# Fusing attention, a dense block and routed experts: keys' neighbour columns by products, turnings at other places, and a new written order

## The chip, the cores and the metric

The kernel runs on one core of one Trainium2 chip. The metric is the device time of one execution in microseconds. A core has five engines with a queue each: TensorE (PE, which loads weights beside its matmuls, PEld), VectorE (DVE), ScalarE (ACT), GpSimd (POOL) and SyncE (SP, which here only issues transfers). Each queue is worked off strictly in its order; semaphores make one engine wait for another or for a transfer.

## The reference, cut to what matters

```python
# 1. attention, 4 batches x 8 heads x 768 positions x 64
k_sum = k.reshape(B, H, 24, 32, D).max(axis=3)       # 24 block keys
v_sum = v.reshape(B, H, 24, 32, D).mean(axis=3)
scores_l = q @ k.T / 8, kept where |i - j| < 16       # a band
scores_s = q @ k_sum.T / 8 + log(32)
a = softmax(concat(scores_l, scores_s));  x = a @ concat(v, v_sum)
# 2. dense block on x as (3072, 512)
h = ((x @ w1) * (x @ w2)) @ w3;  x = h @ w_out
# 3. routed experts, 8 of 512 -> 1024 -> 512
do = x @ w_skip > 0;  e = argmax(x @ w_gate)
out = x;  out[do] += gate * (relu(x @ w1[e]) @ w2[e])
```

The four dense weights come as 64-bit floats, everything else as 32-bit.

## The kernel before, in words

**Stage one** runs from an order written out by hand. `PLAN` holds three strings; each letter is one step, and a step issues its instructions on whichever engines it needs, so the string fixes the order of every queue at once: those of PE, DVE, ACT, POOL and of SP's transfers. The letters that matter below:

- Weights: `f` loads a 512 KB piece of a 64-bit weight (SP; three buffers and one more early on, so a later load waits until a buffer is free), `A` two ACT steps on it, `p`, `i`, `d` one DVE step each, which end in a 32-bit tile; `s` splits it into a high and a low part (ACT copy, DVE difference).
- Folding of `w3 @ w_out` in full precision: `O` turns a tile of `w_out` (four 128x128 transposes), `o` copies it (ACT), `U` multiplies it by the gate columns (four products with 10 columns), `u` splits the result; `X` turns a piece of `w3`, `x` splits it, `F` is 12 matmuls on the split parts, `e` splits their result. The first `F` needs all eight `O`, `U` and `s`.
- Attention, 16 pairs of heads: `k`, `n`, `w`, `m` load keys, queries, values and rows for the block sums (`r`, DVE). `K` turns half of a pair's keys: three whole tiles of 128 positions and the 16 or 32 neighbouring positions that the band needs from the next tile. In its first half the neighbour part comes after the whole tiles, in its second half ahead of them. `h` (ACT) and `H` (DVE) read the result, `Q` and `j` do the same for queries; `S` scores, `a` the softmax, `b` its norm, `T` and `t` turn it, `V` and `v` multiply by the values. `S` and `V` use parts of the TensorE array.
- Dense block: `y` splits x, `B` is 24 matmuls, `g` their product and split, `E` 12 matmuls, `G` the result with the routing, `N` the end of a routing.

The neighbour part is a transpose of few rows, `src[lo:hi, c]` with `ident[lo:hi, lo:hi]` (L140). In both plans each letter stands equally often.

**Stage two** (from L1138, PE's order alone written) is the last three blocks of the dense block, with nothing else on PE.

**Stage three** goes over the experts (`Experts.run`, L887). Each has up to five tiles of 128 tokens; how many is known only when the routing is done, so branches decide. Rows are gathered by POOL (`fetch`), `turn` transposes a gathered tile (four transposes on PE) and splits it (one ACT copy, one DVE difference), `compute` is 24 + 24 matmuls with further turnings at given places (`turns`): ahead of the second layer's matmuls, ahead of their last twelve, and behind these. During an expert's `compute` calls ACT and DVE also split the next expert's weights (`piece`). Expert e's tile 0 is turned during expert e - 1; with more than two tiles, tile 2 is turned at the head of `rest` and its `compute` follows at once.

Of the kernel before, what the change touches and what calls it, by code (L numbers as in the profile page):

```python
# [17 lines left out]
P = 128  # L18
# [37 lines left out]
CUTS0 = (0, 1, 1, 1, 2, 3)  # L56
# [6 lines left out]
class Attention:  # L63
# [58 lines left out]
    def sum(self, i):  # L122
        nc = self.nc
        vt = self.sums.pop(i)
        sm = self.pool.tile([4 * NBLK, D], F32, tag="sm", name="sm", bufs=2)
        for n in (8, 4, 2):
            nc.vector.tensor_add(vt[:, 0:n, :], vt[:, 0:n, :], vt[:, n : 2 * n, :])
        nc.vector.tensor_add(sm, vt[:, 0, :], vt[:, 1, :])
        self.sums["half", i] = sm
        if i % 2:  # L130
            nc.vector.tensor_add(sm, self.sums.pop(("half", i - 1)), self.sums.pop(("half", i)))
            nc.vector.tensor_scalar_mul(self.vs[:, i // 4, i // 2 % 2, :], sm, 1.0 / 32.0)

    def turned(self, name, u, parts):

        src = self.t[name, u]
        f = self.ps.tile([P, 512], F32, tag="tr", name="tr", bufs=1)
        n = 0
        for c, lo, hi in parts:
            self.nc.tensor.transpose(  # L140
                f[:, n : n + hi - lo], src[lo:hi, c, :, :], self.ident[lo:hi, lo:hi]
            )
            n += hi - lo
        self.t[name, "t"] = f

# [132 lines left out]
class AttentionOrder:  # L278
# [20 lines left out]
    def step(self, c):  # L299
# [15 lines left out]
JOBS = "oooooooottttttttwttwttwttwttwwwwwwwwwwww"  # L315
PLAN = (
    (
        "kffAAfpifdpiKmOosAdhAOpUopHifduOsKHUifsrnudohUAQuApiOjdocpiOsUQofsfuApfiAjddSsUpmkiOuofnardSUsOA"
        "AapbiuSomKdphOXHisfdfrQUxTofjAuUbApiXKxuFdmFhpXfAHfiFadrQkjFxeAXppeixAFSdXiaFfpdFwxXFiedtfAbxbpS"
        "VfFeidfvTXAFptAVKaipdvSHiFxedhXnfATFbsxpFKfweXtVAfiAhFpFaHdidfpxvXQmFTeisjFxetbQAjVSdpvAkaFpSfTi"  # L320
        "tiaXFdrxdeKVvSFbAXeffFpHhixnTKFsAtpFfVhAdaHibQXvjdpTQxewijSFAtfpadfibsXeVvdFSxATptifFAVvpXaAFdbi"
        "kTFpdtKViefdxSsXfvewxTnHFAApFhtaFKmpidbissdhVHfvyFTftQsjeVkevr"
    ),
    (
        "QmjAfBSgpABabSiTngaBdpistfSrBgdKAyVpHsgBihdApQbsvigmdBTjfAfKhfrBgBHsypgAmiwdspgBAiQBtafjpkVnbdgs"
        "gSwiBvTAapdBidySQstsgVagrBlgSbBmjbB"
    ),
    (
        "kvgTKBtghHVbEgnQEyvjEKTGtEhHVaESvTrtbBanSVEvGTaEQSmwbtjErbQajNGBGVgvBKglhTmHBwKgtyVvEnTHgrBtVhES"
        "babQvESEgGaTBEtSEVgGjvbkBNgKhBHTlGEkQtVEgvjETnKGyaEGBHhgEtBbEgSmGEBaSVvawENEBgSQbjBKggTBtHaVEvTh"  # L330
        "GrBQgGbEwtVjKByvhHSggBgEBabQTGSkgaBtSEnjKVEhHvTKaHhmtEbBbQVGEvTEjgtVrSvaENkBSGGTwgBabtKgVSvgHhBT"
        "QbgmBtyjgbEQVajBKkvETtEBVgHhSBgvEanTSGEtVrbaEvKTgBbtSGVEvhHNBkmgKEhwTGGtBVHgabvgQjBTEQgBjbytVSgn"
        "BvagSETGtBKEBrEagwgSBhVHQGBEjgKBHbEvgNhkEgwbGaBBgEEybgTnQBtjGEGBVSEKvEgTtaESEGVBagvbTESgEtbNHBVh"
        "vBgTGGwQjEtKgBVanhHQgvBbTByjgtSBaSgVBQgvbaESBTjEQGajtgEEVGkKhHvbBKhNgEEwTHgEtSaVvbBSGTGbtBVagBvg"
        "TgBtbgVvSETEtVvEaTGbtEEVGEvTEtVvENGG"
    ),
)

# [359 lines left out]
class Experts:  # L698
# [188 lines left out]
    def run(self, pool, ps, early):  # L887
        tc, nc = self.tc, self.nc
        self.pool, self.ps = pool, ps
        cj = pool.tile([P, 1], I32, name="cj")  # L890
        manual = lambda: tc.manual_schedule(engines=ENGINES)
        with tc.If(early < P):
            with manual():
                self.fetch(0, 0)
                self.turn(self.place(0, 0), ps)
        with tc.If(early < 2 * P):
            with manual():
                self.fetch(0, 1)
        def state():
            return self.done, self.loaded, dict(self.raws), list(self.free)  # L900

        def soon(label, n, least):

            tc.mark_branch_hint_location(label, hint=n >= least, engines=[PE])

        def rest(e):

            at, bt = self.place(e, 2), self.place(e, 3)
            with tc.If(ns[e] > 2, label=f"three{e}"):
                with manual():  # L910
                    soon(f"four{e}", ns[e], 4)
                    self.turn(at, ps)
                    self.compute(self.col(e, 2), e, at, (None, bt))
                with tc.If(ns[e] > 3, label=f"four{e}"):
                    with manual():
                        soon(f"five{e}", ns[e], 5)
                        self.compute(self.col(e, 3), e, bt)
                    with tc.If(ns[e] > 4, label=f"five{e}"):
                        with tc.For_i(4, ns[e], 1) as j:
                            nc.vector.tensor_copy(cj, self.idx[:, bass.ds(j + e * NTILE, 1)])  # L920
                            self.gather(cj, at[0])
                            self.turn(at, ps)
                            self.compute(cj, e, at)

        ns = None
        for e in range(E):
            more = e + 1 < E
            first, own, nxt = self.place(e, 0), self.place(e, 1), self.place(e + 1, 0) if more else None
            with manual():
                if e == 0:  # L930
                    for z, j in ((1, 0), (0, 2), (1, 1), (2, 0), (2, 1), (1, 2)):
                        self.fetch(z, j)
                    self.compute(self.col(0, 0), 0, first, (None, own, nxt), CUTS0)
                else:
                    for z, j in ((2, 0), (2, 1), (1, 2)):
                        self.fetch(e + z, j)
            if ns is None:
                ns = [nc.values_load(self.nt[0:1, z : z + 1], min_val=0, max_val=NTILE) for z in range(E)]
            half, whole = (HALF, CUTS) if more else ((), ())

            before = state()
            with tc.If(ns[e] > 1, label=f"two{e}") as many:  # L944
                with manual():
                    soon(f"three{e}", ns[e], 3)
                    self.fetch(e, 3)
                    if e:
                        self.compute(self.col(e, 0), e, first, (own, nxt), half)
                rest(e)  # L950
                with manual():
                    if more:
                        soon(f"two{e + 1}", ns[e + 1], 2)
                    self.compute(self.col(e, 1), e, own, (None, None), half)
            after = state()
            self.done, self.loaded, self.raws, self.free = before[0], before[1], dict(before[2]), list(before[3])
            with many.Else():
                with manual():
                    if more:
                        soon(f"two{e + 1}", ns[e + 1], 2)  # L960
                    if e:
                        self.compute(self.col(e, 0), e, first, (None, nxt), whole)
                    else:
                        for _ in range(sum(HALF)):
                            self.piece(PIECES)
            now = state()
            assert now[:2] == after[:2] and list(now[2]) == list(after[2])
            assert [id(t) for t in now[3]] == [id(t) for t in after[3]]
# [252 lines left out]
```

## Time and profile before

| | us |
|---|---|
| median of 3 runs | 859.61 (859.29 to 861.21) |
| the profiled execution's own time | 858.83 |
| its span, first to last instruction | 857.0 |

Shares of the span: PE 95%, PEld 87%, DVE 60%, ACT 53%, POOL 12%. The profiled execution's own time is 1.83 us over its span. A timeline row names the start, the length, the engine, the line, the instruction, what it writes and reads, the count of like instructions merged into the row, and in brackets how long the engine had been idle and who ended that. Since matmuls overlap, their price is read from one start to the next, not from their lengths.

### The profile page before, as it was taken

To read this page: it belongs to the slowest core of one execution; us is meant where nothing else is said; L and a number is where in the kernel's file an instruction comes from. 1 tells how busy PE (TensorE), PEld (TensorE's weight loads), DVE (VectorE), ACT (ScalarE), POOL (GpSimd) and SP (SyncE) were. 2 spreads that over 40 slices of the span, in tenths; PEclk is the share of its full clock that TensorE was granted. 3 is DMA by queue.
4 is the path that set the end of the run, shared out by engine and by line. 5 is a ranking of instruction groups with operands and counts; after the bars stand their busy time and mean duration, and the time that the engine had idled before them with its cause. 6 is when DMAs were issued, how large, how long until landed. Compare 5 with 4: busy or idle time off the path is not lost. (4 is left out here: it accounts for less than half of the span.)

```text
span 857.0 us, 18400 instructions
## 1 busy us (share of the span) xinstructions
PE 816.4 (95%) x6882; PEld 743.4 (87%) x6882; DVE 513.8 (60%) x1684; ACT 452.3 (53%) x1235; POOL 102.5 (12%) x136
## 2 busy tenths in 40 slices
PE   3799999999999999999999999999998999998996
PEld 3689988999999999999999989999996787776775
DVE  4889998976664547566455555642354285165952
ACT  4768998766554445444334445522244274265851
POOL 1000000000110001010001010200215114022320
PEclk9999999999999999999999999999999899999999
DMA  8677877553506243233222322510136266055910
GB/s 239 170 196 192 220 186 194 160 125 81 140 10 133 63 97 89 70 87 63 60 69 61 61 41 70 183 69 22 63 111 228 104 234 213 16 184 178 332 69 21
DMA packets 124615, 105.07 MB, mean 123 GB/s; under 512 B 92914, under 2 KB 98082, under 8 KB 124496
## 3 DMA queue, kind: packets, MB, share of 16 engines
q1 hardware_dynamic: 120144, 98.04, 41.1%
q0 software_dynamic: 4352, 5.51, 2.0%
q8 instruction: 67, 1.10, 0.6%
q14 instruction: 52, 0.43, 0.2%
HBM read 90.45 MB, written 16.64 MB: 125 GB/s over the span
## 5 line engine op out<-in xcount | busy, mean ns | idle before, releaser
L573 PE MATMUL x2p<-wh,slab 128*128 128x266 f32 (+1 forms) x768 | 157.0, 291 | 0.0
L573 PEld LDWEIGHTS x2p<-wh,slab 128*128 128x128 f32 x768 | 124.1, 189 | 3.0 <-issue 1.7
L573 PE MATMUL x2p<-wl,slab 128*128 128x256 f32 (+1 forms) x384 | 109.0, 284 | 0.0
L224 ACT ACTIVATE pr<-pr,st 128x120 f32<-128x120 f32 x192 | 73.5, 386 | 41.7 <-DVE st L214 41.6
L530 PE MATMUL ab<-slab,wB1h 128*128 128x256 f32 x384 | 73.6, 290 | 0.6 <-DVE slab L547 0.6
L530 PE MATMUL ab<-slab,wA1h 128*128 128x256 f32 x384 | 73.4, 288 | 0.2 <-DVE slab L388 0.2
L552 DVE TENSOR_TENSOR a<-a,ab 128x256 f32<-128x256 f32 x84 | 35.2, 419 | 63.4 <-ACT a L543 62.9
L573 PEld LDWEIGHTS x2p<-wl,slab 128*128 128x128 f32 x384 | 72.7, 189 | 0.0
L530 PE MATMUL ab<-slab,wB2h 128*128 128x256 f32 x384 | 70.8, 282 | 0.0
L530 PE MATMUL ab<-slab,wA2h 128*128 128x256 f32 x384 | 70.3, 281 | 0.0
L553 ACT ACTIVATE slab<-a 128x256 fp32r<-128x256 f32 x84 | 35.0, 417 | 64.2 <-DVE a L552 63.7
L543 ACT ACTIVATE a<-ab 128x256 f32<-128x256 f32 x96 | 36.4, 379 | 60.2 <-PE ab L530 57.7
L530 PEld LDWEIGHTS ab<-slab,wA1h 128*128 128x128 f32 x384 | 59.0, 189 | 2.2 <-issue 0.6
L530 PEld LDWEIGHTS ab<-slab,wB1h 128*128 128x128 f32 x384 | 58.8, 190 | 1.5 <-DVE slab L547 0.8
L554 DVE TENSOR_TENSOR slab<-a,slab 128x256 fp32r<-128x256 f32 x84 | 36.4, 433 | 38.7 <-ACT slab L553 38.7
L530 PEld LDWEIGHTS ab<-slab,wB2h 128*128 128x128 f32 x384 | 59.1, 190 | 0.0
L530 PEld LDWEIGHTS ab<-slab,wA2h 128*128 128x128 f32 x384 | 58.9, 189 | 0.0
L530 PE MATMUL ab<-slab,wA1l 128*128 128x256 f32 x192 | 54.0, 281 | 0.0
L530 PE MATMUL ab<-slab,wB2l 128*128 128x256 f32 x192 | 53.9, 281 | 0.0
L530 PE MATMUL ab<-slab,wA2l 128*128 128x256 f32 x192 | 53.9, 281 | 0.0
L530 PE MATMUL ab<-slab,wB1l 128*128 128x256 f32 x192 | 53.9, 281 | 0.0
L828 ACT ACTIVATE hr<-hp 128x512 f32<-128x512 f32 x30 | 18.0, 599 | 64.3 <-PE hp L824 64.1
(176 smaller groups left out, 2087.1 us busy)
## 6 DMA issues: line engine op xcount, KB each, us to landing
eraw<-in_moe_w SPq DMA_DIRECT2D x64, 512.0 KB
raw<-in_moe_w SPq DMA_DIRECT2D x32, 512.0 KB
vaug<-in_v SPq DMA_DIRECT2D x32, 240.0 KB
x2e<-row SPq DMA_DIRECT2D x24, 256.5 KB
kn<-in_k SPq DMA_DIRECT2D x32, 192.0 KB
vt<-in_v SPq DMA_DIRECT2D x16, 384.0 KB
qn<-in_q SPq DMA_DIRECT2D x32, 192.0 KB
out<-row SPq DMA_DIRECT2D x24, 256.0 KB
```

Of the source, the lines that this page charges most:

```text
L224: nc.scalar.activation(pr[:, i, :], pr[:, i, :], AF.Exp, scale=-1.0, bias=st[:, 0, i : i + 1], accum_out=st[:, 1, i : i + 1],)
L530: self.nc.tensor.matmul(pp[:, s, :], l[:, c, fs], r[:, c, :], start=(c == 0 and j == 0), stop=(c == 3 and j == 2),)
L543: nc.scalar.activation(a, pp[:, 0, :], AF.Copy)
L552: nc.vector.tensor_mul(a, a, pp[:, 1, :])
L553: nc.scalar.activation(gh[:, f % 4, :], a, AF.Copy)
L554: nc.vector.tensor_sub(gl[:, f % 4, :], a, gh[:, f % 4, :].bitcast(F32))
L573: self.nc.tensor.matmul(po[:, 0 : hi - lo], l[:, f, s * P : s * P + P], r[:, 4 * h + f, lo:hi], start=(h == 0 and f == 0 and j == 0), stop ...
L828: nc.scalar.activation(hr, hps[s], AF.Relu)
```

## The change

It has three parts. In `turned`, the neighbour part of the keys becomes a product of the whole tile with 16 or 32 columns of the identity. In `Experts.run`, the tile turned at the end of expert 0's first `compute` is its own tile 2 (no longer expert 1's tile 0), and `rest` of expert 0 no longer turns it; and the next expert's tile 0 is turned in the last `compute` of an expert with several tiles, no longer in its first. `PLAN` is written anew, all three strings, with the same number of each letter.

```diff
         for c, lo, hi in parts:
-            self.nc.tensor.transpose(
-                f[:, n : n + hi - lo], src[lo:hi, c, :, :], self.ident[lo:hi, lo:hi]
-            )
+            if hi - lo == P:
+                self.nc.tensor.transpose(f[:, n : n + P], src[:, c, :, :], self.ident)
+            else:
+                self.nc.tensor.matmul(
+                    f[:, n : n + hi - lo], src[:, c, :, :].rearrange("p a d -> p (a d)"), self.ident[:, lo:hi], start=True, stop=True
+                )
             n += hi - lo
 PLAN = (
     (
-        "kffAAfpifdpiKmOosAdhAOpUopHifduOsKHUifsrnudohUAQuApiOjdocpiOsUQofsfuApfiAjddSsUpmkiOuofnardSUsOA"
-        "AapbiuSomKdphOXHisfdfrQUxTofjAuUbApiXKxuFdmFhpXfAHfiFadrQkjFxeAXppeixAFSdXiaFfpdFwxXFiedtfAbxbpS"
...
+        "fAfkKfApipdimfhdHOrfoAnfKUhOupoidssOsApUiHoudfAcApUOipdoiusQsmfUjkdfAQOjpiuodfSfsarUuOSApoaASiOb"
+        "mUdKnpHishoudUsAfOXrpuoAipdTfUixKduXFFxXAFpHiAdmfhQrpxieAXfjpFdkfxetQAawFXibFdxFjpSFeAabXSKiVpdf"
...
     ),
...
                     soon(f"four{e}", ns[e], 4)
-                    self.turn(at, ps)
+                    if e:
+                        self.turn(at, ps)
                     self.compute(self.col(e, 2), e, at, (None, bt))
...
-                    self.compute(self.col(0, 0), 0, first, (None, own, nxt), CUTS0)
+                    self.compute(self.col(0, 0), 0, first, (None, own, self.place(0, 2)), CUTS0)
...
-                        self.compute(self.col(e, 0), e, first, (own, nxt), half)
+                        self.compute(self.col(e, 0), e, first, (own, None), half)
                 rest(e)
...
-                    self.compute(self.col(e, 1), e, own, (None, None), half)
+                    self.compute(self.col(e, 1), e, own, (None, nxt), half)
...
                     else:
+                        self.turn(nxt, ps)
                         for _ in range(sum(HALF)):
                             self.piece(PIECES)
```

## Rows read from the trace of the kernel before

**Rows 1.** The page's first part: busy time, share of the span, instructions of each engine.
```profile
PE 816.4 (95%) x6882; PEld 743.4 (87%) x6882; DVE 513.8 (60%) x1684; ACT 452.3 (53%) x1235; POOL 102.5 (12%) x136
```

**Rows 2.** Stretches: length, busy time (instructions) of PE, PEld, DVE, ACT, POOL, clock, DMA, GB/s.
```profile
5.10:51.60 46.50, 33.63 (x181) 28.69 (x182) 34.14 (x87) 30.35 (x75) 0.72 (x1) 1.00 0.70 207
51.60:160.00 108.40, 105.00 (x1083) 96.52 (x1082) 98.93 (x288) 92.86 (x257) 4.38 (x9) 1.00 0.76 196
160.00:543.00 383.00, 380.74 (x3854) 360.86 (x3853) 224.53 (x944) 189.53 (x625) 26.46 (x47) 1.00 0.33 79
...
647.90:857.00 209.10, 192.91 (x900) 153.60 (x900) 110.18 (x172) 102.38 (x187) 54.49 (x49) 0.98 0.47 159
```

**Rows 3.** PE in order of time, its first two steps.
```profile
5.16 1.09 PE L140 MATMUL tr<-ident,kn 128*128 128x128 f32 x4 [5.16 <-DMA kn<-in_k]
10.85 1.11 PE L409 MATMUL wot<-ident,nt 128*128 128x128 f32 x4 [4.60 <-DVE nt L380]
```

**Rows 4.** SP's first transfers, in order of time.
```profile
1.19 1.00 SPq L89 DMA_DIRECT2D kn<-in_k  x2
2.23 2.06 SPq L356 DMA_DIRECT2D raw<-in_moe_w_out  x4
```

**Rows 5.** ACT's first step on a weight.
```profile
8.13 0.66 ACT L364 ACTIVATE nt<-raw 128x512 f32<-128x512 f32 x1 [6.12 <-DMA raw<-in_moe_w_out]
```

**Rows 6.** PE in order of time, `U` and what follows it, in the first stretch.
```profile
45.61 1.72 PE L424 MATMUL up<-wsg,wt 128*128 128x10 f32 x8
47.17 1.09 PE L244 MATMUL tp<-ident,pr 128*120 128x128 f32 x4
```

**Rows 7.** PE in order of time, from the first `F` on.
```profile
51.62 0.57 PE L454 MATMUL po<-oh,th 128*128 128x266 f32 x1
...
55.49 0.41 PE L454 MATMUL po<-oh,tl 128*128 128x256 f32 x1
55.71 0.41 PE L454 MATMUL po<-oh,th 128*128 128x256 f32 x1
...
56.12 0.28 PE L454 MATMUL po<-oh,tl 128*128 128x256 f32 x1
56.24 0.28 PE L454 MATMUL po<-oh,th 128*128 128x256 f32 x1
...
56.60 0.60 PE L409 MATMUL w3t<-ident,nt 128*128 128x128 f32 x4
56.95 0.37 PE L454 MATMUL po<-oh,th 128*128 128x266 f32 x1
```

**Rows 8.** PE in order of time, around a first half of `K`.
```profile
222.78 0.65 PE L140 MATMUL tr<-ident,kn 128*128 128x128 f32 x4
223.36 0.65 PE L244 MATMUL tp<-ident,pr 128*120 128x128 f32 x4
```

**Rows 9.** PE in order of time, around a second half of `K`.
```profile
353.44 0.28 PE L530 MATMUL ab<-slab,wA2l 128*128 128x256 f32 x1
353.65 0.72 PE L140 MATMUL tr<-ident,kn 32*128 32x32 f32 x4
354.13 0.37 PE L573 MATMUL x2p<-wh,slab 128*128 128x266 f32 x1
```

**Rows 10.** PE in order of time, from expert 0's tile 0 to its tile 2.
```profile
659.97 0.39 PE L848 MATMUL yp<-wA2l,hth 128*128 128x512 f32 x1
660.19 0.39 PE L848 MATMUL yp<-wA2h,htl 128*128 128x512 f32 x1
662.28 0.63 PE L804 MATMUL xt<-ident,xg 128*128 128x128 f32 x4 [1.70 <-DMA xg<-x2e,idx]
664.06 1.09 PE L804 MATMUL xt<-ident,xg 128*128 128x128 f32 x4 [1.15 <-issue]
665.84 0.79 PE L824 MATMUL hp<-ea0h,exh 128*128 128x512 f32 x1 [0.69 <-ACT exh L387]
```

**Rows 11.** Stretch with the lower clock, columns as in Rows 2.
```profile
665.80:670.50 4.70, 4.67 (x11) 3.45 (x12) 0.93 (x2) 0.00 (x0) 2.64 (x3) 0.50 0.93 327
```

More of the change, by code (lines that the diff above doesn't have):

```diff
@@ L317 @@
     (
-        "kffAAfpifdpiKmOosAdhAOpUopHifduOsKHUifsrnudohUAQuApiOjdocpiOsUQofsfuApfiAjddSsUpmkiOuofnardSUsOA"
-        "AapbiuSomKdphOXHisfdfrQUxTofjAuUbApiXKxuFdmFhpXfAHfiFadrQkjFxeAXppeixAFSdXiaFfpdFwxXFiedtfAbxbpS"
-        "VfFeidfvTXAFptAVKaipdvSHiFxedhXnfATFbsxpFKfweXtVAfiAhFpFaHdidfpxvXQmFTeisjFxetbQAjVSdpvAkaFpSfTi"
-        "tiaXFdrxdeKVvSFbAXeffFpHhixnTKFsAtpFfVhAdaHibQXvjdpTQxewijSFAtfpadfibsXeVvdFSxATptifFAVvpXaAFdbi"
-        "kTFpdtKViefdxSsXfvewxTnHFAApFhtaFKmpidbissdhVHfvyFTftQsjeVkevr"
-    ),
@@ L324 @@
-    (
-        "QmjAfBSgpABabSiTngaBdpistfSrBgdKAyVpHsgBihdApQbsvigmdBTjfAfKhfrBgBHsypgAmiwdspgBAiQBtafjpkVnbdgs"
-        "gSwiBvTAapdBidySQstsgVagrBlgSbBmjbB"
-    ),
-    (
[L329 to L335, printed above, removed]
+        "fAfkKfApipdimfhdHOrfoAnfKUhOupoidssOsApUiHoudfAcApUOipdoiusQsmfUjkdfAQOjpiuodfSfsarUuOSApoaASiOb"
@@ new lines @@
+        "mUdKnpHishoudUsAfOXrpuoAipdTfUixKduXFFxXAFpHiAdmfhQrpxieAXfjpFdkfxetQAawFXibFdxFjpSFeAabXSKiVpdf"
+        "iFexvdfAnfTtpFaXShFibHdbAVxeFvpsiQeXTfdjxFtVAAKvaXFFpHwFpiiddxfhesmTAbfXpetQixjFAdfVpSvaArFXikTS"
+        "taFbVFdfpvSbKxfeXATipndextFiAhHFmpFwVfavdiQXjfrFesfKxhTHtVQdmAfpvbiFTApdjStiXVedsxFvkAapfAfFrSaX"
+        "TibdxeKptShwAapHFfFiidedbVvsXATpnFxtKisVmdhAFpfHviFsQdTfyjtsQjVebfSeB"
+    ),
+    (
+        "ArpvigABTdBpgBaisdySgtAgBsnpkaSiVbKfwAvfpdiHBTgshgAfdQpjtfaiBdbQBsVyjgfKAHpigvwdshlBATpgBtisgnBA"
+        "BpdQidsVygSsbaBgSBbkgm"
+    ),
@@ new lines @@
+    (
+        "avgkBSrTmtBgbjVgQjEKyEwvETtEVGEhHvaKHhGTbtBErSVEnvaNSEKaTGGgBblmShHBtVgvQgjBTQEgbjKtHEEVyBvThErn"
+        "atGSVgQaBSbBgvTmatbBwGVSkEgvjKTgHkEhtNElbKEVHGvEhTEQnrGytEjaBgwSbaVGmBBvgTSntEQBaVSgwvbBajgEKEgH"
+        "GEkNBTghEbtBGKBrEhHgVgQEvjTGSytaESVnabBvTSbQjGgtBKEVEkHghGvKBTatbhENHBkVQvETjSgtEnabKgBVGGvgSBTa"
+        "gBSmBbygtHVhaQBbrwjvgETKHtBEgVhvQgETtjESGmaVBbKGkwbSaBESgvNhEHEGTgtKhEnHQVGavBTtbgBVBvjTgrQBytgB"
+        "nbjmSgEVvEaQSaBETrSjgktEKgHhGwbBgVKBvGHEgwBghBTbtENgaBVBgQjGgEKvSEaTGtbESEEyGaVBvESgGTtBVBHEgbvh"
+        "KEbNEHhgBEQjgTGBGQgBjatngbBVvgBTEyStVgBavTEbStGVEvQwTatSjBgVQbEvkEjKTgtBaGNHgbEBGwEhgVKEvBhHTSGg"
+        "BtagVSabBvgBSTEgtbVvaEETEGtVbEGvNEGETtEVvG"
```

## The prediction

> **What bounds the kernel now.** The page's first part comes first: PE is busy for 816.4 of 857.0 us, the next engine, DVE, for 513.8 [rows 1]. The table of stretches then shows where PE is not full [rows 2]. From 160 to 543 it lacks 2.3 us in 383, so there only shorter PE work helps. From 51.6 to 160 it lacks 3.4 of 108.4, and DVE (98.93) and ACT (92.86) come close. In the first 46.5 us it lacks 12.9, with DVE at 34.14 and ACT at 30.35: no engine is full, they wait for one another. The experts' stretch lacks 16.2 us, part of it the tail behind the last matmul, which no edit touches. PE's first rows in order of time say what is late early on: it waits 5.16 us for the first keys and then 4.60 for the last DVE step on a weight [rows 3].
>
> One more thing is seen only in PE's timeline. Matmuls of 256 columns start 0.22 us apart until about 56.0 us and 0.12 apart from 56.1 on [rows 7]: TensorE ran at 1.2 GHz until then and at 2.4 after (the clock column says 1.00 for both, since no record covers the first stretch). The rise came 4.5 us after the first F, which started at 51.62. So the time of the first F counts: behind it PE is full and fast nearly to the end, and each us by which it comes earlier is a us of the total.
>
> **Neighbour columns by products.** Four whole tiles take 0.35 at the full clock, from 56.60 to the matmul at 56.95 [rows 7]. I read this as 0.11 from one to the next and 0.02 from the last to the matmul. A first half of K takes 0.58 from start to start [rows 8]. Three whole tiles are 0.33 of that, so the small one costs 0.25. A second half takes 0.48 with a matmul behind it, where three whole tiles would take 0.24, and the step ahead of it is 0.21, from 353.44 to 353.65 [rows 9], where matmuls of that size stand 0.12 apart [rows 7]: 0.24 + 0.09 = 0.33. There are 16 of each: 16 x 0.25 + 16 x 0.33 = 9.3 us.
>
> The trace has no such product. The nearest row is U: four products with 10 columns appear as eight records and take 1.56 us from 45.61 to 47.17 at the lower clock [rows 6], so 0.39 a product. Matmuls there cost nearly twice what they cost later [rows 7], so I take half at the full clock, 0.195; times 32 that is 6.2. One thing is given back. S and V use parts of the array like the small transpose, and I take it that they too cost 0.09 more behind a step with whole tiles. Behind a small transpose this was already paid, and it no longer will be. Counting letters, the old order pays it 74 times and the new one 79 times, 4 of these behind such a half: 5 x 0.09 = 0.45. So 9.3 - 6.2 - 0.45 = **2.6 us less**. Ends: 5.3 less if a product costs no more than a whole tile (0.11), 3.4 more if the clock doesn't help it (0.39). Four of the 32 stand ahead of the first F, where little is won.
>
> The Trainium skill, "FP8 and Floating Point Precision" (TensorE Precision Notes), says that true FP32 takes four passes through the array. If each pass cost what a whole tile does, a product would be 0.44 and this edit 32 x 0.44 - 9.3 + 0.45 = 5.2 us more instead of 2.6 less. The trace shows two records to a product, not four [rows 6], and so speaks against the rule as a price.
>
> **The new order, until the first F.** SP used to issue two transfers of keys from 1.19 and the first four weights from 2.23 [rows 4]. ACT could start on a weight at 8.13, 5.9 us after the issue [rows 5]. The new string begins f, A, f, k, k..: two weights go ahead of the keys. The first is issued at 1.19, and lands between 5.2, when the keys arrived that had this place [rows 3], and 7.1, the same 5.9 us after issue. I take the middle, 6.1: ACT and DVE start 2 us earlier. In exchange the keys land about when the first weight did, at 8, and K, still PE's first step, ends near 9.2. The first O then needs A, p, i and d, and in the new string p of the second weight stands between; the old chain took 10.85 - 8.13 = 2.7 [rows 3, 5], so the O follows K without loss. Up to the first F the new order has the same eight O and U, four K and three S. It has one Q, j, b, x and A less, and one d more. So from the first landing to the first F the work is the same, 51.62 - 8.13 = 43.5 us, and the F comes at 49.6, 2.0 us earlier. DVE stood idle for about 9 of these 43.5 (34.14 busy, nothing before the landing) [rows 2]. A better interleave could win up to half of that, 4.5 more; I take 0.5. **2.5 us less**, with ends of 6.5 less and 5.5 more (the last rival). SP's other transfers (queries, values, later weights) move with their letters; I take them at nothing.
>
> **The order after the first F.** The work of each letter is the same. Between 51.6 and 160 the three engines are all above 85%, and from 160 on PE lacks next to nothing, so a stall can go or come for a us at most: taken as nothing, ends 2 less and 2 more. What hides K's edit on PE is gone if ACT or DVE bind until 137; ten of 32 K lie there, at most 0.8 of the 2.6.
>
> **Turnings of the experts.** Behind expert 0's tile 0, PE waits until 662.28 for the first gather, turns expert 1's tile, meets the branch and turns tile 2 at 664.06, waits 0.69 for its split and starts the matmuls at 665.84 [rows 10]. Now the second gather is turned in the first place. It was issued behind the first (POOL's order is as before) and had landed by 664.06, so the turning starts between 662.3 and 664.1. The branch then lies beside the split. With 0.63 for the turning [rows 10] and the larger of 0.69 and 1.15 behind it, the matmuls start between 664.1 and 665.9, and I take 664.6, 1.2 earlier. At that point the clock is at 1.2 GHz (0.50 from 665.8 to 670.5 [rows 11]), so half of it is won, 0.6. Expert 1's turning (0.35 at the full clock) is still to be paid later, and has become no cheaper. This leaves about **0.3 us less**, ends 1.5 less and 0.7 more. The other moves put one turning (four transposes, one ACT copy, one DVE difference; no transfer) from an expert's first `compute` into its last, with twelve matmuls behind it as cover (12 x 0.22 = 2.6 us by the starts at 659.97 and 660.19 [rows 10], against a split of which PE waited 0.69 for the first half): nothing.
>
> **Sum.** 2.6 + 2.5 + 0.3 = 5.4 off the profiled execution's own 858.83: 853.4. The median shown lies 0.8 above that execution, so 854.2; I say 854.
>
> **Rivals.**
> - *The order gains all it can.* DVE's idle time in the first stretch is halved and some waits after 60 us go: 6.5 and 1.0 in place of 2.5, with 2.6 and 0.3: 859.6 - 10.4 = 849.2. For: no engine is full there. Against: every step in that stretch crosses engines, and the waits are many and short.
> - *The early gain is given back.* The first F is earlier, but ACT and DVE, at 86 and 91% until 160, set the pace, and K's ten early halves save nothing: 859.6 - 1.8 - 0.3 = 857.5. For: their busy shares. Against: PE is at 97% there.
> - *Products cost more than what they replace.* Where their price is set by something that doesn't follow the clock, it stays at 0.39: 859.6 + 3.4 - 2.8 = 860.2. For: no row shows one at the full clock. Against: every other PE row there nearly halves. The rule of four passes (the Trainium skill, the page above) would make it 859.6 + 5.2 - 2.8 = 862.0.
> - *A slower start.* The first weight lands no earlier, because what it waits for is not the keys ahead of it; the keys then come behind two weights, at 11 or later, and K, the first O and every U behind it move back; the rise of the clock moves with the first F. With an F at 57, 5.5 later, and the other parts as forecast, 859.6 + 5.5 - 2.9 = 862.2. It decides from an F later than 54.5 (2.9 behind 51.6). For: PE does its queue in order, and K is still its first step. Against: the keys, at the head, took 4.0 us, and the first weight behind them 5.9.
>
> **Chances.** Forecast 0.50, all gains 0.15, given back 0.17, products 0.07, slower start 0.11. About 0.2% (1.7 us) is what a measurement of this kernel can tell from no change. Faster by that, under 857.9: the first two, the forecast's own spread aside, and most of the third, 0.79. Slower, over 861.3: 0.11, the last. Same: 0.10, the products and the slow edge of the third. The range 849.5 to 860.0 leaves out half of the all-gains case, half of the products and the slower start; the forecast alone is 851.5 to 856.5.
>
> **What would show it.** K's halves at full clock: 0.52 in place of 0.58 from start to start, and no gap of 0.21 ahead of a second half. The products of 16 or 32 columns as two records, 0.2 together; 0.4 makes that step wrong. ACT's first weight step near 6.1, and the first F at 49 or before; an F after 51.6 makes the second step wrong even if the time is right. The pitch of 0.12 should set in some 4 to 5 us behind that F. In the experts, expert 0's tile 2 should start its matmuls within 4.5 us of the end of tile 0's, against 5.65 now (660.19 to 665.84). The prediction as a whole is wrong if PE's busy time doesn't fall, or if PE's idle time from 51.6 on grows by what the start wins.

## The result, and the profile after

The changed kernel takes 845.88 us (median of 4 runs, 845.26 to 848.43) against 859.94 for the kernel before in the same comparison: 14.1 us less, ratio 0.984 [0.982, 0.986]. The forecast was 5.4 less. The profiled execution took 845.26 with a span of 843.5, against 858.83 and 857.0. Lines of the kernel after stand 3 higher than before from L143 on.

The page's first part, as [rows 1]: PE is busy for 8.8 us less, DVE and ACT hardly differ.

```profile
PE 807.6 (96%) x6914; PEld 742.9 (88%) x6914; DVE 512.1 (61%) x1684; ACT 453.0 (54%) x1235; POOL 105.4 (13%) x136
```

The table of stretches, columns as in [rows 2]. The third stretch is the surprise: PE lacks 0.17 us of 383, where it lacked 2.26. The last row begins with the experts' first matmul, 7.2 us earlier than before (640.71 against 647.88), and its clock column is 1.00 where it was 0.98.

```profile
5.10:51.60 46.50, 32.90 (x184) 29.94 (x185) 33.79 (x86) 29.03 (x72) 0.42 (x1) 1.00 0.73 204
51.60:160.00 108.40, 104.92 (x1107) 97.93 (x1107) 101.82 (x303) 96.47 (x269) 7.10 (x9) 1.00 0.78 204
160.00:543.00 383.00, 382.83 (x3920) 366.58 (x3919) 225.87 (x954) 190.93 (x625) 28.36 (x49) 1.00 0.33 82
640.70:843.00 202.30, 190.05 (x900) 151.87 (x900) 110.25 (x172) 102.33 (x187) 54.99 (x49) 1.00 0.49 164
```

SP's first transfers, as [rows 4], then ACT's first step, as [rows 5]: the first weight is there at 4.97, 3.2 us earlier than before and 1.1 earlier than I took.

```profile
1.19 0.89 SPq L359 DMA_DIRECT2D raw<-in_moe_w_out  x2
2.12 1.02 SPq L89 DMA_DIRECT2D kn<-in_k  x2
...
4.21 0.84 SPq L119 DMA_DIRECT2D vt<-in_v  x1
```
```profile
4.97 0.66 ACT L367 ACTIVATE nt<-raw 128x512 f32<-128x512 f32 x1 [2.96 <-DMA raw<-in_moe_w_out]
```

Then DVE and PE in order of time, as [rows 3]. The keys come at 9.66 and the first `O` at 10.62, where the old one stood at 10.85. DVE then meets `r`, the block sums, and waits 4.57 us for rows of the values that SP had asked for at 4.21. The weights behind `r` in DVE's queue wait with it, so PE's third `O` stands at 20.41 after an idle time of 4.46.

```profile
16.68 1.46 DVE L127 TENSOR_TENSOR vt<-vt 96x512 f32<-96x512 f32 x3 [4.57 <-DMA vt<-in_v]
```
```profile
9.66 0.88 PE L141 MATMUL tr<-ident,kn 128*128 128x128 f32 x3 [9.66 <-DMA kn<-in_k]
10.33 0.45 PE L143 MATMUL tr<-ident,kn 128*128 128x16 f32 x2
10.62 1.09 PE L412 MATMUL wot<-ident,nt 128*128 128x128 f32 x4
...
20.41 1.09 PE L412 MATMUL wot<-ident,nt 128*128 128x128 f32 x4 [4.46 <-DVE nt L383]
...
51.13 0.57 PE L457 MATMUL po<-oh,th 128*128 128x266 f32 x1
...
52.60 0.43 PE L457 MATMUL po<-oh,th 128*128 128x266 f32 x1
52.82 0.39 PE L457 MATMUL po<-ol,th 128*128 128x266 f32 x1
53.05 0.29 PE L457 MATMUL po<-oh,tl 128*128 128x266 f32 x1
53.17 0.29 PE L457 MATMUL po<-oh,th 128*128 128x266 f32 x1
```

So the first `F` comes at 51.13, only 0.5 us earlier than in [rows 7]. But the pitch (the time from one matmul's start to the next) falls from 0.22 to 0.12 at 53.05, 1.9 us behind it, where it was 4.5. Below, "the rise" is this step of TensorE's clock from 1.2 to 2.4 GHz; its time is the start of the first entry in the trace's clock record.

A first half of `K` at the full clock (as [rows 8]) and a second half (as [rows 9]): from start to start 0.47 in place of 0.58, and 0.43 in place of 0.48, with no gap of 0.21 ahead of the second. The product is two records, and a pair takes 0.14 or 0.15.

```profile
211.02 0.49 PE L141 MATMUL tr<-ident,kn 128*128 128x128 f32 x3
211.35 0.29 PE L143 MATMUL tr<-ident,kn 128*128 128x16 f32 x2
211.49 0.63 PE L247 MATMUL tp<-ident,pr 128*120 128x128 f32 x4
...
348.77 0.60 PE L247 MATMUL tp<-ident,pr 128*120 128x128 f32 x4
349.20 0.31 PE L143 MATMUL tr<-ident,kn 128*128 128x32 f32 x2
349.35 0.53 PE L141 MATMUL tr<-ident,kn 128*128 128x128 f32 x3
349.63 0.48 PE L533 MATMUL ab<-slab,wA1h 128*128 128x256 f32 x2
```

Expert 0 between its tile 0 and its tile 2, as [rows 10]. One turning, two waits of 0.9 and no branch between them: 2.8 us from the last matmul of one tile to the first of the next (653.03 to 655.82), where it was 5.65. The matmuls that follow stand 0.23 to 0.33 apart: the clock column is 1.00 here, where [rows 11] had 0.50.

```profile
653.03 0.39 PE L851 MATMUL yp<-wA2h,htl 128*128 128x512 f32 x1
654.31 0.63 PE L807 MATMUL xt<-ident,xg 128*128 128x128 f32 x4 [0.90 <-DMA xg<-x2e,idx]
655.82 0.49 PE L827 MATMUL hp<-ea0h,exh 128*128 128x512 f32 x1 [0.88 <-ACT exh L390]
656.15 0.40 PE L827 MATMUL hp<-ea0l,exh 128*128 128x512 f32 x1
656.38 0.47 PE L827 MATMUL hp<-ea0h,exl 128*128 128x512 f32 x1
```
```profile
655.80:660.50 4.70, 4.68 (x21) 3.68 (x22) 2.36 (x4) 1.41 (x3) 2.65 (x3) 1.00 0.99 380
```

### The profile page after: what moved, and what is told of

The parts are those of the page before. It is cut to its first block, busy times and chain, and to the rows that moved or that the text cites. A ratio compares the mean times of both kernels' runs of the same rounds, so it can differ in the third digit from the quotient of the medians.

```text
span 843.5 us, 18460 instructions
## 1 busy us (share of the span) xinstructions
PE 807.6 (96%) x6914; PEld 742.9 (88%) x6914; DVE 512.1 (61%) x1684; ACT 453.0 (54%) x1235; POOL 105.4 (13%) x136
```

## Where the profiled 13.6 us went

Up to the experts' first matmul the time is the first `F`, half of the stretch at the lower clock behind it, PE's idle time from 51.6 to 160 and from 160 to 543 us, and the rest, which is PE's work at the full clock and the 0.8 us for which it stands idle between 543 us and the experts in both kernels. Before: 51.62 + 4.47/2 + 3.40 + 2.26 + 588.4 = 647.9. After: 51.13 + 1.91/2 + 3.48 + 0.17 + 585.0 = 640.7. So of the 7.2 us the `F` itself is 0.5, the earlier rise 1.3, waits 2.0 and shorter work 3.4. The profile of the order alone (below) has 587.65 in the last place, so 2.7 of the 3.4 are the products and 0.7 the order's packing, a remainder that I can't put down to lines. From the experts' first matmul to the end of the span it is 6.3 less (209.1 to 202.8). By the third `compute` 4.9 of that is won: it starts 28.53 us behind the first, where it started 33.47 behind. The rest is mostly waits later in the stretch: two of before, 1.3 us at 793.3 and 1.0 at 838.8, are not there, and one of 1.42 at 785.2 has become 1.84 at 774.0.

## The experiments

Theory: the three parts act apart from each other; expert 0's gap and the lower clock behind it are the part that I undersized, and waits behind 160 us are what I didn't see in the order. Rivals: the whole gain hangs on the earlier weights; the parts only work together; one long wait around 510 us is what the order removes.

| kernel | median us | runs | before | ratio, interval |
|---|---|---|---|---|
| products | 857.34 | 12 | 859.60 | 0.997 [0.995, 0.999] |
| order | 855.53 | 7 | 859.60 | 0.993 [0.991, 0.996] |
| turns | 855.45 | 8 | 859.60 | 0.995 [0.993, 0.997] |
| turns0 | 855.31 | 10 | 859.60 | 0.994 [0.992, 0.996] |
| late_sum | 845.04 | 6 | 859.68 | 0.984 [0.981, 0.986] |
| weights_first | 858.67 | 12 | 859.68 | 0.999 [0.998, 1.001] |
| filled_before | 858.90 | 12 | 859.68 | 1.000 [0.998, 1.002] |
| filled_after | 845.62 | 6 | 859.68 | 0.986 [0.982, 0.990] |
| changed_again | 847.04 | 4 | 858.84 | 0.987 [0.986, 0.989] |
| without_products | 848.90 | 4 | 858.84 | 0.989 [0.987, 0.990] |
| without_order | 853.81 | 6 | 858.84 | 0.994 [0.992, 0.996] |
| without_turns | 850.39 | 5 | 858.84 | 0.991 [0.989, 0.992] |
| early_max | 859.12 | 12 | 859.43 | 1.000 [0.998, 1.002] |
| best | 844.62 | 5 | 859.43 | 0.983 [0.981, 0.985] |
| changed_third | 845.42 | 6 | 859.43 | 0.985 [0.982, 0.987] |

Kernels with the same median of before shared its runs.

### Each part alone

**products**: the kernel before with the edit in `turned` only (the first hunk of the diff ahead).

```diff
-            self.nc.tensor.transpose(
-                f[:, n : n + hi - lo], src[lo:hi, c, :, :], self.ident[lo:hi, lo:hi]
+                self.nc.tensor.matmul(
+                    f[:, n : n + hi - lo], src[:, c, :, :].rearrange("p a d -> p (a d)"), self.ident[:, lo:hi], start=True, stop=True
```


> The kernel before with the neighbour columns as products and nothing else. By the theory that each part of the change pays for itself (PE's shorter steps count wherever PE is full): K's halves go from 0.60 and 0.52 us to 0.51 and 0.49, the 0.09 ahead of a second half goes, some 3 us less, 857.0, with the first F still near 51.6. Rival, that only the new order pays: ACT and DVE set the pace until 137 and waits take the rest, under 1 us less, 859 or more.

Measured 2.3 less. Its profiled execution was its longest (861.68), and shows what a short wait can cost in the middle of the kernel. In PE's order of time, 2.06 us of waiting end at 511.79; some matmuls later the pitch is 0.22, and the trace's clock is at its lower level from 513.05 to 516.46. It is there from 181.96 to 185.37 too, beside waits of 0.61 and 0.97 us that end at 180.39 and 182.04.

```profile
511.79 0.64 PE L201 MATMUL sp<-kaug,qT 64*64 64x120 f32 x16 [2.06 <-POOL kaug L176]
512.36 0.69 PE L261 MATMUL ov<-pt,vaug 120*64 120x64 f32 x16
512.98 0.76 PE L533 MATMUL ab<-slab,wB1h 128*128 128x256 f32 x2
513.53 0.42 PE L533 MATMUL ab<-slab,wB1l 128*128 128x256 f32 x1
513.75 0.63 PE L533 MATMUL ab<-slab,wB1h 128*128 128x256 f32 x2
```

**order**: the kernel before with the new `PLAN` only.

```diff
-        "kffAAfpifdpiKmOosAdhAOpUopHifduOsKHUifsrnudohUAQuApiOjdocpiOsUQofsfuApfiAjddSsUpmkiOuofnardSUsOA"
...
+        "fAfkKfApipdimfhdHOrfoAnfKUhOupoidssOsApUiHoudfAcApUOipdoiusQsmfUjkdfAQOjpiuodfSfsarUuOSApoaASiOb"
...
```


> The kernel before with the new written order and nothing else. By the theory that each part pays for itself: about 4 us less, 856, of which 1.5 from TensorE's clock, which rises about 2 us behind the first F instead of 4.5, and 2 from waits between 160 and 543 that go; the small transposes still cost their 9 us. Rival, that the order carries nearly all of the 14: 849 or less. Rival, that it only moves waits about: within 1 us of before.

Measured 4.1 less. Its first `F` is at 51.20, the rise 2.5 us behind it, PE's idle time from 160 to 543 us 0.07, and the experts' first matmul at 643.33, 4.6 earlier than in the kernel before. By the formula above that is 0.4 for the `F`, 1.0 for the rise, 2.4 for waits and 0.7 for packing. The clock still falls in expert 0 (661.2 to 668.1).

**turns** and **turns0**: the kernel before with the moved turnings only; in the second only those around expert 0, the other experts' tile 0 being turned in the first `compute` as before.

```diff
-                    self.turn(at, ps)
+                    if e:
+                        self.turn(at, ps)
...
-                    self.compute(self.col(0, 0), 0, first, (None, own, nxt), CUTS0)
+                    self.compute(self.col(0, 0), 0, first, (None, own, self.place(0, 2)), CUTS0)
```


> The kernel before with the moved turnings of the experts and nothing else. By the theory that the gap behind expert 0's tile 0 and TensorE's lower clock behind it cost 5 us together: its matmuls of tile 2 start 15.1 us after those of tile 0 (18.0 before), the clock stays at 2.4 GHz, 854.5. My prediction's reading, that the lower clock stays as it was: 0.3 less, 859.6.

> As the run with the moved turnings alone, but only expert 0's are moved; experts 2, 3 and 6 turn the next expert's tile in their first call, as before. If the gap and the clock at expert 0 are the cause: the same time as with all moved, within 1 us, 854.5 to 855.5. If lighter first calls of the other experts matter (less for ACT and DVE to do there): half of the gain, 857.

Measured 4.1 and 4.3 less: the whole effect sits in expert 0, and the other moves are worth nothing that can be seen, as forecast. Rows of turns0: one wait of 1.05 for the branch remains, and matmuls stand 0.43 apart for 3 us. Its clock is at the lower level from 663.43 to 666.84, half as long as the 6.83 us of the kernel before (663.66 to 670.49).

```profile
661.99 0.63 PE L804 MATMUL xt<-ident,xg 128*128 128x128 f32 x4 [0.98 <-DMA xg<-x2e,idx]
663.67 0.79 PE L824 MATMUL hp<-ea0h,exh 128*128 128x512 f32 x1 [1.05 <-issue]
664.26 0.63 PE L824 MATMUL hp<-ea0l,exh 128*128 128x512 f32 x1
664.68 0.63 PE L824 MATMUL hp<-ea0h,exl 128*128 128x512 f32 x1
```

### Each part taken out of the changed kernel

> The changed kernel once more, as the measure for the three runs beside it. 845.9 as at first, between 844.5 and 847; mean clock about 0.997.

**without_products**, the first hunk undone:

```diff
-            if hi - lo == P:
-                self.nc.tensor.transpose(f[:, n : n + P], src[:, c, :, :], self.ident)
-            else:
...
+            self.nc.tensor.transpose(
+                f[:, n : n + hi - lo], src[lo:hi, c, :, :], self.ident[lo:hi, lo:hi]
```


> The changed kernel with the neighbour columns as small transposes again. If the three parts add up: 2.4 to 3 us more than the changed kernel, 848.6. If the new order's savings need the shorter steps (or hide them): 1 us more or less than that, 847 or 850.

**without_order**, the old `PLAN` back:

```diff
-        "fAfkKfApipdimfhdHOrfoAnfKUhOupoidssOsApUiHoudfAcApUOipdoiusQsmfUjkdfAQOjpiuodfSfsarUuOSApoaASiOb"
...
+        "kffAAfpifdpiKmOosAdhAOpUopHifduOsKHUifsrnudohUAQuApiOjdocpiOsUQofsfuApfiAjddSsUpmkiOuofnardSUsOA"
...
```


> The changed kernel with the old written order. If the parts add up: 4 to 6 us more than the changed kernel, 851. If the gains overlap in the lower clock (a wait fewer matters only when TensorE's clock falls behind it): less than 4, 849 or under.

**without_turns**, all turnings back:

```diff
-                    self.compute(self.col(0, 0), 0, first, (None, own, self.place(0, 2)), CUTS0)
+                    self.compute(self.col(0, 0), 0, first, (None, own, nxt), CUTS0)
...
-                    self.compute(self.col(e, 1), e, own, (None, nxt), half)
+                    self.compute(self.col(e, 1), e, own, (None, None), half)
```


> The changed kernel with the turnings of the experts where they were. If the parts add up: 4 to 5 us more than the changed kernel, 850.3, with the gap behind expert 0's tile 0 back (over 17 us from its first matmul to tile 2's) and the mean clock back at 0.995. If the new order alone moves the gather's landing so that the gap closes by itself: under 2 us more.

Against changed_again they cost 1.9, 6.8 and 3.3, in sum 12.0, and the whole change won 11.8 in that comparison. The three parts alone win 10.5 in sum, of 14. Only the products' 1.9 is inside the intervals. So most of each part's gain comes without the others. That they act wholly apart isn't shown: the order is worth 4.1 alone and 6.8 undone, over the 4 to 6 that I expected, while the products and the turnings come in under what I expected of them undone. In without_order PE waits 2.12 us at 509.85, and the clock falls from 511.54 to 514.95; in without_turns it falls from 656.2 to 663.0, and again from 779.1 to 782.5.

```profile
509.85 0.64 PE L201 MATMUL sp<-kaug,qT 64*64 64x120 f32 x16 [2.12 <-POOL kaug L176]
```

The order's effect stands in every profile kept, not only in one pair. "New" below is the order as it is in the diff; "old" takes in early_max and weights_first, which move one letter of it. PE's idle time is read from the same stretch as in [rows 2].

| order | profiles | first `F` | rise | PE idle, 160 to 543 | experts' first matmul |
|---|---|---|---|---|---|
| old, small transposes | 6 | 51.57 to 51.95 | 53.18 to 56.09 | 1.3 to 2.8 | 647.5 to 648.7 |
| old, products | 2 | 51.31, 51.47 | 54.16, 55.66 | 4.3, 4.7 | 649.4, 651.4 |
| new, small transposes | 2 | 50.78, 51.20 | 52.52, 53.66 | 0.1, 0.1 | 642.6, 643.3 |
| new, products | 5 | 49.50 to 51.13 | 48.01 to 53.52 | 0.2 | 639.6 to 640.7 |

So the waits between 160 and 543 us go with the old order each time, and products lengthen them: the wait for `kaug` near 510 is 2.06 and 2.12 us with products and 1.15 to 1.32 in the small-transpose profiles that have it. This fits the order's larger worth beside the products; two profiles are few for it.

The profile of changed_again contradicts one of my readings: here the rise (48.01 by the clock record) lies ahead of the first `F`, and from its second matmul on the pitch is 0.13, not 0.22.

```profile
48.56 0.39 PE L143 MATMUL tr<-ident,kn 128*128 128x32 f32 x2
48.78 0.53 PE L141 MATMUL tr<-ident,kn 128*128 128x128 f32 x3
49.15 0.60 PE L412 MATMUL w3t<-ident,nt 128*128 128x128 f32 x4
49.50 0.37 PE L457 MATMUL po<-oh,th 128*128 128x266 f32 x1
49.71 0.29 PE L457 MATMUL po<-ol,th 128*128 128x266 f32 x1
49.84 0.29 PE L457 MATMUL po<-oh,tl 128*128 128x266 f32 x1
```

### The start

**late_sum**: the changed kernel with `r` behind the third weight's `d`; only DVE's order changes.

```diff
-        "fAfkKfApipdimfhdHOrfoAnfKUhOupoidssOsApUiHoudfAcApUOipdoiusQsmfUjkdfAQOjpiuodfSfsarUuOSApoaASiOb"
+        "fAfkKfApipdimfhdHOfoAnfKUhOupoidrssOsApUiHoudfAcApUOipdoiusQsmfUjkdfAQOjpiuodfSfsarUuOSApoaASiOb"
```


> The changed kernel with one letter moved: the first block sum (r) stands behind the third weight's last DVE step instead of ahead of its first. Theory: in the changed kernel DVE stands 4.6 us still for the rows of that sum, which land at 16.7, and PE waits 4.5 us for the third O; with the letter moved that wait goes, the third O starts about 17.1 instead of 20.4, and the first F at 48.5 instead of 51.1: 2 to 2.5 us less than the changed kernel, 844. Rival: later waits (1.4 us at 36.9, 1.9 at 43.4) grow by as much, the first F stays at 51, and the time is the changed kernel's, 846.

**weights_first**: the kernel before, two weights ahead of the first keys.

```diff
-        "kffAAfpifdpiKmOosAdhAOpUopHifduOsKHUifsrnudohUAQuApiOjdocpiOsUQofsfuApfiAjddSsUpmkiOuofnardSUsOA"
+        "ffkAAfpifdpiKmOosAdhAOpUopHifduOsKHUifsrnudohUAQuApiOjdocpiOsUQofsfuApfiAjddSsUpmkiOuofnardSUsOA"
```


> The kernel before with its first two loads of weights ahead of the first keys (ffk for kff), nothing else. My prediction's step: ACT starts 2 to 3 us earlier, at 5 instead of 8.1, nothing else stands in the way since its order needs the sum's rows much later, and the first F comes 2 us earlier, at 49.5: 857.6 against 859.6. Rival, that the start is bound by the exchange between engines and not by the landing: first F at 51 or later, no gain.

In late_sum, `r` starts at 16.60 without waiting, the wait ahead of the third `O` is 1.32, and the first `F` stands at 48.16, against 51.13, 49.50 and 50.74 in three profiles of the changed kernel. So the block sums held the start up. In weights_first ACT starts on a weight at 4.85, as early as in the changed kernel, and the first `F` is at 51.95, no earlier than before: earlier weights by themselves bring nothing here. The keys, now behind two weights, are used at 10.18, and `K` stands ahead of the first `O` in PE's queue, so that `O` starts at 11.20, no earlier than the 10.85 of [rows 3].

```profile
16.74 1.11 PE L412 MATMUL wot<-ident,nt 128*128 128x128 f32 x4 [1.32 <-DVE nt L383]
...
48.16 0.57 PE L457 MATMUL po<-oh,th 128*128 128x266 f32 x1
...
653.96 0.50 PE L827 MATMUL hp<-ea0h,exh 128*128 128x512 f32 x1 [2.60 <-ACT exh L390]
```
```profile
4.85 0.66 ACT L364 ACTIVATE nt<-raw 128x512 f32<-128x512 f32 x1 [2.84 <-DMA raw<-in_moe_w_out]
```

The 3.0 us of late_sum are still there at the experts' start (637.99, 2.7 earlier), but its median is only 0.8 under that of the changed kernel in its first comparison, with nearly the same interval. In its profile they go in expert 0: PE waits 2.60 for ACT's split (above), the clock falls from 654.99 to 658.40, and the third `compute` starts at 669.13, against 669.24 in the changed kernel.

### Is it the clock in expert 0?

**filled_before**: the kernel before with seven matmuls more behind expert 0's tile 0, and **filled_after**: the changed kernel with four there and three behind the turning. Their results are read by nobody.

```diff
+            w = ps.tile([P, 512], F32, tag="xt", name="warm", bufs=2)
+            for _ in range(7):
+                nc.tensor.matmul(w, xh[:, 0, :], ah[0][:, 0:512], start=True, stop=True)
```


> The kernel before with seven matmuls more ahead of expert 0's third turning, of the expert's own operands, into a PSUM tile that nobody reads: they fill PE's wait of 1.7 us for the gather. Theory: TensorE's clock falls behind that wait, and the lower clock costs 2 to 2.5 us by itself; filled, the clock stays at 2.4 GHz, tile 2's matmuls start at the same time or 0.2 later, and tile 1's come 2 us earlier: 857.5. Rival, that the clock falls by what comes later there (two more waits of 1.15 and 0.69) or that the wait itself is all the cost: 859.6 or 0.2 more.

> The changed kernel with four such matmuls ahead of expert 0's turning of tile 2 and three behind it, where PE waits 0.9 and 0.9 us. Theory: in some executions of the changed kernel the clock still falls there (mean clock 0.995 instead of 0.999, up to 3 us more); filled, it falls in none: median 0.5 to 1 us under the changed kernel's, 845, and a narrower spread. Rival: the matmuls delay the turning and the branch behind it, 0.5 us more, 846.5.

In the profile of filled_before the matmuls fill the first wait, the clock doesn't fall in the experts (1.00 from 665.8 to 670.5, where [rows 11] had 0.50), and the third `compute` starts 31.54 us behind the first, against 33.47.

```profile
660.24 1.79 PE L875 MATMUL warm<-ea0h,exh 128*128 128x512 f32 x7
661.87 1.22 PE L804 MATMUL xt<-ident,xg 128*128 128x128 f32 x8
664.68 0.50 PE L824 MATMUL hp<-ea0h,exh 128*128 128x512 f32 x1 [1.59 <-ACT exh L387]
...
666.34 0.50 PE L824 MATMUL hp<-ea0h,exl 128*128 128x512 f32 x1 [0.93 <-DVE exl L388]
```
```profile
665.80:670.50 4.70, 4.16 (x19) 3.39 (x20) 0.48 (x1) 0.60 (x1) 2.21 (x3) 1.00 0.76 267
```

Yet over 12 runs the time is the same, 1.000 [0.998, 1.002]. One profile shows 1.9 us at the third `compute`; the runs don't show them at the end. Each run's mean granted clock (1 is 2.4 GHz all through, from the rise on) says why: the profiled execution, the fastest of the 12, had 0.998, but the median is 0.995, where the kernel before has 0.994. The six runs at 0.996 or more have a median of 857.5, the six at 0.994 or less one of 861.0. So the filling kept the clock up in about half of the executions only. filled_after didn't do what was expected either: its six runs lie between 843.61 and 853.37, a wider spread than the changed kernel's, with mean clocks from 0.992 to 0.999.

With the turnings moved, alone, the mean clock is 0.996 or more in 15 of 18 runs (turns and turns0), against 5 of the 24 of the kernel before. The medians are 0.997 and 0.994; by my estimate the difference, 0.003 of 857 us, is some 2.6 of the 4.1 us. The mean doesn't say where the clock fell, but the profiles do:

| turnings | profiles | gap, tile 0 to tile 2 | third `compute` behind the first | lower clock in expert 0 |
|---|---|---|---|---|
| where they were, nothing filled | 6 | 3.61 to 5.65 | 31.2 to 34.6 | in all 6, 3.4 us in two and 6.8 in four |
| moved, nothing filled | 9 | 2.28 to 3.66 | 28.0 to 31.1 | in 3 (turns0, late_sum, best), 3.4 us each |

The medians are 4.7 and 3.05 for the gap, 33.3 and 29.3 for the third `compute`. The kernel before has the longest gap of all, so that one pair of profiles, 5.65 against 2.8, shows more than is typical. So the moved turnings shorten the gap and, in most executions, keep the clock up, and turns0 shows that expert 0's alone are enough. That the clock would make the gain without the shorter gap isn't shown.

### One long wait, and a better order

**early_max**: the kernel before, with the last `H` ahead of `N`, so that POOL's step for the last `S` is ready sooner.

```diff
-        "vBgTGGwQjEtKgBVanhHQgvBbTByjgtSBaSgVBQgvbaESBTjEQGajtgEEVGkKhHvbBKhNgEEwTHgEtSaVvbBSGTGbtBVagBvg"
+        "vBgTGGwQjEtKgBVanhHQgvBbTByjgtSBaSgVBQgvbaESBTjEQGajtgEEVGkKhHvbBKhHNgEEwTgEtSaVvbBSGTGbtBVagBvg"
```


> The kernel before with one letter moved near the end of its attention: the last keys' maximum (H) right behind their copy (h), ahead of the routing step (N), so that GpSimd copies the block keys before it issues the two scatters of the routing. Theory, that the order's gain is made of such waits and of what they do to the clock: PE's wait of 1.2 to 2.1 us near 510 goes, and with it the fall of the clock that followed it in two of the profiles (3.4 us at half speed): 1.2 to 3 us less than before, 857 to 858. Rival, that the wait is given back at the next one: no change.

The kernel before waits 1.32 us at 509.82 for POOL's `kaug`; here the `S` doesn't wait, and the step behind it does, for ACT, 0.79 us. The time is the same, 1.000 [0.998, 1.002]. So this wait, of which 0.79 came back one step later, doesn't carry the order's gain; no other was tried by itself.

```profile
508.57 0.64 PE L198 MATMUL sp<-kaug,qT 64*64 64x120 f32 x16
510.00 0.69 PE L258 MATMUL ov<-pt,vaug 120*64 120x64 f32 x16 [0.79 <-ACT pt L250]
```

**best**: the changed kernel with `r` later, as in late_sum, one split ahead of a softmax, and one copy earlier.

```diff
-        "fAfkKfApipdimfhdHOrfoAnfKUhOupoidssOsApUiHoudfAcApUOipdoiusQsmfUjkdfAQOjpiuodfSfsarUuOSApoaASiOb"
-        "mUdKnpHishoudUsAfOXrpuoAipdTfUixKduXFFxXAFpHiAdmfhQrpxieAXfjpFdkfxetQAawFXibFdxFjpSFeAabXSKiVpdf"
+        "fAfkKfApipdimfhdHOfoAnfKUhOupoidrssOsApUiHoudfAcApUOipdoiusQsmfUjkdfAQOjpiuodfSfasrUuOSApoaASiOb"
+        "mUodKnpHishudUsAfOXrpuoAipdTfUixKduXFFxXAFpHiAdmfhQrpxieAXfjpFdkfxetQAawFXibFdxFjpSFeAabXSKiVpdf"
```


> The changed kernel with four letters moved in its first fifth: the first block sum behind the third weight's last DVE step (as in the run late_sum), and for the two waits that were left ahead of the first F (1.4 us for a softmax, 1.9 for a copied tile of w_out) the softmax step ahead of a split, and the copy ahead of the keys' turning. Theory: the first F comes at 45 to 46 instead of 51 or 48, and each us of it counts: 842.5 to 844. Rival: what is won there is lost at the experts, whose first gather's wait is set by the transfers then: 845, as late_sum.

> The changed kernel again, as the measure for the run best on the same chip: 846 to 847.

Its first `F` is at 48.20, the same as late_sum's: the two further moves shift a wait (3.04 us for `S` at 35.60, where late_sum has 1.39 at 33.92) and win nothing. At 844.62 it beats the kernel before clearly, and the changed kernel in the same comparison by 0.8, within the intervals.

## Why the prediction was wrong, point by point

**The turnings, forecast 0.3, measured 4.1 alone and 3.3 undone.** This step of the sum was mis-sized. The mechanism stood as written: the second gather is turned first, the branch goes beside the split. The forecast start, 664.6 in place of 665.84, made the gap 4.4 us; it is 2.8. (The bracket took 662.28 as the earliest turning, 14.4 us behind the experts' first matmul; it starts 13.6 behind it here.) And I halved the gain because the clock would stay low, and charged a moved turning, where in all three profiles of the changed kernel the clock didn't fall in the experts' stretch until the tail, and in turns and turns0 the mean clock of most runs is higher. So the term that was wrong is the lower clock, taken as unchanged. [Rows 11] was in front of me as a cost of 4.7 us at half speed; I took it as a given and didn't ask what it came from.

**The start, forecast 2.5 by an earlier first F.** This step failed as put. The first weight came even earlier than forecast, but the first `F` only 0.5, 2.1 and 0.9 us earlier in three profiles. The keys were taken to land at 8 and land at 9.66, so the first `O` starts at 10.62 and not at 9.2. And "SP's other transfers ... I take them at nothing" was the mistake that cost the `F`: `r` had moved ahead of the third weight in DVE's queue, and the rows it reads land at about 16.6. late_sum shows it: with `r` later the `F` is at 48.16, though the keys are used no earlier than 9.14. The sign that I named (an `F` after 49) says the same.

**The order after the first F, forecast nothing, ends of 2.** This is as large a part of the error as the turnings: order alone is worth 4.1, undone 6.8, and by the profile of order 0.4 of it is the `F`. "A stall can go or come for a us at most" was wrong twice. The stretch from 160 to 543 had 2.3 us of waits, in [rows 2], and all but 0.2 went, in each profile of the new order. And a wait there can cost more than its length: in profiles of products and without_order the clock falls right behind such waits for 3.4 us each, 1.7 lost. How the order's gain splits over runs between waits, the clock and the earlier rise isn't settled: early_max took the largest wait of the stretch and got nothing. Falls of the clock are at most a small part of it in the kernel before: the median of the runs' mean clocks is 0.994 there and 0.995 in order, some 0.9 us by the same estimate as for the turnings.

**The rise behind the first F.** Read from [rows 7] as following the `F`; in changed_again and filled_after it came ahead of it (48.01 and 48.34 against 49.50 and 49.60). With that, "each us of an earlier `F` is a us of the total" has lost its reason. In late_sum it held up to the experts (3.0 us earlier, 2.7 left there) and no further.

**The products, forecast 2.6, measured 2.3 alone and 1.9 undone** (2.7 by the work up to the experts). Right in direction and signs: a pair takes about 0.15, not 0.195, and no gap of 0.21 is left. That the number came out is in part luck. With 0.145 for a pair the same sum gives 9.3 - 4.6 - 0.45 = 4.2, and a part of what was lost again lies in the halves beside `V`: a second half behind `V` takes 0.52 in the changed kernel, where the small transpose in the profile of order takes 0.48 and has no 0.09 ahead of it. The interval of products, 0.5 to 4.3 us less, can't tell 2.6 from 4.2. (The end "3.4 more" was mis-added, too: 32 x 0.39 - 9.3 + 0.45 is 3.6.) The Trainium skill, "FP8 and Floating Point Precision" (TensorE Precision Notes), counts four passes for true FP32. As a price that isn't borne out here: two records, 0.14 to 0.15 for the pair, little more than one whole tile at 0.11.

**Rivals.** Of the four, "the order gains all it can" came nearest, though by waits behind 160 us and not by the start. Products that cost more, and a slower start, are out. The gain given back occurred in late_sum and best, in expert 0 and not before 160.

## What to carry to other kernels

Before a rebuilt order is priced by its first steps, look up for each step that moves forward in an in-order queue when the transfer it reads lands; one that is late holds everything behind it. Where one engine is full for hundreds of us, add up its short waits over the whole stretch, and look at the clock behind each: they are a term of the sum, not noise. Undo parts from the full change as well as trying them alone, and don't trust one wait in one profile: two experiments here removed a wait or a fall of the clock that the profile showed, and the time stayed. The mean granted clock of every run tells whether the profiled execution is a typical one.

## What the runs showed of the hardware that I had not expected

The granted clock can fall behind waits as short as 0.6 and 1.0 us close together (products, at 182 us), and it doesn't always: without_order has waits of 0.45 and 0.97 us at the same place, ending at 180.55 and 182.20, and keeps the full clock from the rise to 511.54. The same program differs in this between executions: the changed kernel lost the clock for 3.4 us behind a wait of 1.86 at 118.7 in one profile and in two others nowhere between the rise and the tail, and its rise came 1.5 us ahead of the first `F` in one and 1.9 and 2.8 behind it in the others. A load of the values for the block sums, issued at 4.21, was first used at 16.68 by an engine that waited for it, 12.5 us later, where the first weight took 3.8 us from issue to use.
